# Stage two in nine chunks of 512 tokens, and seven own buffers for the last layer's values

## The chip, the cores and the metric

The kernel runs on one NeuronCore of one Trainium2 chip. The metric is the device time of one execution, in microseconds (us). Five engines matter: TensorE (PE; its weight loads are listed apart as PEld), VectorE (DVE), ScalarE (ACT), GpSimd (POOL) and SyncE (SP), which here issues most of the DMA transfers in the order of its queue.

## What is computed

Linear attention with random features over 8 batches, 8 heads and 576 tokens of 64 numbers, and a gated layer on its output, 4608 tokens of 512 numbers:

```python
def phi(x):                                   # x of q or k, scaled by D**-0.25
    h = np.einsum('bhsd,md->bhsm', x, omega) - np.sum(x * x, axis=-1, keepdims=True) / 2.0
    return np.exp(h - np.max(h, axis=-1, keepdims=True)) / np.sqrt(m)
kv  = np.einsum('bhsm,bhsd->bhmd', k_p, v);  z = np.sum(k_p, axis=2)
num = np.einsum('bhsm,bhmd->bhsd', q_p, kv)
den = np.einsum('bhsm,bhm->bhs', q_p, z)[..., None] + 1e-06
x   = (num / den).transpose(0, 2, 1, 3).reshape(4608, 512)
out = (1 / (1 + np.exp(-(x @ w_gate))) * (x @ w_val)) @ w_out   # 512 -> 1536 -> 512
```

## The kernel before

Every product of the gated layer is made of three matmuls: each operand is split into a rounded high part and the rest (a low part), and high x high, high x low and low x high are added up in PSUM. The high part is a copy by ScalarE, the low part a subtraction by VectorE or GpSimd.

Stage one holds the attention and, interleaved with it by a planner, the first 4 of the 12 column tiles of the gated layer (line 531), in chunks of 512 tokens, the first of them in two of 256. There the weights `wh`, `wl` are the stationary operand and the tokens `xe` the moving one. Results go to DRAM as `ye`, the attention's output as `xT`.

Stage two (`second_pass`, line 689) does the other 8 column tiles, in 4 pairs, by a seven-product scheme for 2 x 2 blocks (Strassen-Winograd). It runs over `NCW` = 6 chunks of `NW` = 768 tokens, in two halves of `W` = 384. For each pair there are two groups (`kind` 0 the gate, 1 the value), so n = 0 to 7 in a chunk. A group (`gated`, line 615) is seven products of six matmuls at line 631, stationary `units` (weights, `u`), moving `x` (token sums, `xl`), 128 x W each, in three of the eight PSUM banks. PE's order is 1, 6, 5 of a group, then 4, 3 of the group before (`held`), then 2, 7 of the group. Between the products stand their sums out of PSUM: line 645 copies the first result to `p1`, line 613 adds on VectorE (`u2` after product 6, `u3` and one more after product 7, one each after 4 and 3), lines 639 and 654 are the sigmoids, line 652 the one multiplication on VectorE, which comes once per pair. Products 2, 7, 4 and 3 write again into banks from which a sum has to be read first. After a pair's second group GpSimd makes seven operations (line 680) for the seven operands of the last layer, and two DMAs (line 687, `put`) store them to `yl`, issued by SP in the next pair's second group.

The next chunk's seven operands are made during a chunk by `operands` (line 582): four loads into `xr` when n = 1 is done, and then sums (line 591), high parts (line 577) and low parts (line 580) at places written out as (chunk, n, slot); most of them come at n = 7 and at n = 0 of the chunk itself. There are eight buffers for them (`buffer`, line 432): seven in the pool `late`, one in the pool `tail`. In the last chunk the units of the last layer are loaded as the units of stage two come free (line 442, one per group from n = 1 to n = 6), and `first_values` puts the loading and splitting of the first token group's values there.

The last layer (`last`, line 777) goes over 18 token groups of 2 x 128 tokens. For each of six pairs j it takes raw values of 128 x 896 (`gated_values`: for j below 2 three loads from `ye`, line 734, and four sums, line 741; otherwise one load from `yl`, line 736), splits them (`parts_of`, lines 749 and 751) into `yh` and `yl`, which lie `APART` floats into two of the same eight buffers, and runs 21 matmuls at line 800, stationary `yh`/`yl`, moving `u`, 128 x 256. So a group has 126. Raw values sit in buffers of the tags `xr` and `ya`, two of each, shared with stage two; of the first group's six, the last four are in a buffer of the tag `u`. The first matmuls of group 0 run ahead of products 4 and 3 of stage two's last group. At the end of each token group line 816 copies a result and line 613's sums give the output.

`BELOW`, `APART` and the tiles that nothing uses move tiles in memory by so many floats.

Of the kernel before, what the change touches and what calls it, by code (L numbers as in the profile page):

```python
# [9 lines left out]
F32 = mybir.dt.float32  # L10
# [10 lines left out]
P = 128  # L21
# [14 lines left out]
NC = 512  # L36
Q = NC // 2
NCH = B * S // NC
W = 3 * P
NW = 2 * W  # L40
NCW = B * S // NW
SUB = W // P
NJ = DF // P
NPAIR = NJ // 2
# [7 lines left out]
BANKS, PAIRS = 4, 2  # L52
XK = 6
XL, XE = 7, 1
UL, UE = 5, 3


BELOW, APART = 80, 80

FILL = 1e6  # L60

# [25 lines left out]
N_OPS = 7  # L87
# [142 lines left out]
def attn_glu_kernel(ctx: ExitStack, tc, qT, kT, qn, kn, va, om, ident, w, out):  # L230
# [30 lines left out]
    def any_bank(name):  # L261

        n_banks[0] += 1
        return bank(n_banks[0] % 8, name)
# [5 lines left out]
    def pin(ins):  # L270
        return tc.keep_in_program_order(ins) if pinned else ins
# [39 lines left out]
    def after(event, t):  # L311
        while event.left:
            yield event
        return max(t, event.time)
# [4 lines left out]
    def dve(n):  # L319
        return (n + 65) / 0.96  # L320
# [10 lines left out]
    def dma(t, kb, n=1):  # L331

        turns.free["SP"] = t + n * ISSUE
        moved[0] = max(moved[0], t + n * ISSUE + LANDS) + kb * 3.2
        return moved[0]
# [94 lines left out]
    turn_of = [0]  # L430

    def buffer(name):
        at, n = (late, XL) if turn_of[0] % (XL + XE) < XL else (tail, XE)
        turn_of[0] += 1
        return at.tile([P, 2, 2, W], F32R, tag="x", bufs=n, name=name)

    def unit(pool, n):
# [144 lines left out]
    def operands(c, x):  # L582

        xr = [tail.tile([P, 2, NW], F32, tag="xr", bufs=2, name=f"xr{c}_{i}") for i in range(2)]
        for k in range(KC):
            pin(nc.sync.dma_start(out=xr[k // 2][:, k % 2], in_=xT[k, :, c * NW : (c + 1) * NW]))
        (a11, a21), (a12, a22) = ((r[:, :, :W], r[:, :, W:]) for r in xr)
        s = late.tile([P, 2, W], F32, tag="s", bufs=1, name=f"s{c}")

# [25 lines left out]
    def gated(c, x, pair, kind, g, ya, yb):  # L615
# [3 lines left out]
        wh, wl = units[2 * (pair - EP) + kind]  # L619
        b0, b1, b2 = (any_bank(f"gw{i}_{id_}")[:, :W] for i in range(3))  # L620
        v0, v1, v2 = (b.rearrange("p (s t) -> p s t", s=SUB) for b in (b0, b1, b2))
# [101 lines left out]
        assert not plan  # L723
        return held

    def gated_values(g, j, raw=None):

        if raw is None:
            raw = tail.tile([P, 8, P], F32, tag=("xr", "ya")[j % 2], bufs=2, name=f"yr{g}_{j}")
        t = g // SUB * NW + g % SUB * P  # L730
        if j < EP:
            one, two, both = ye[j, :, 1, t + W : t + W + P], ye[j, :, 0, t + W : t + W + P], ye[j, :, :, t : t + P]
            for to, x in ((raw[:, :2], both), (raw[:, 2], one), (raw[:, 7], two)):
                pin(nc.sync.dma_start(out=to, in_=x))
        else:
            pin(nc.sync.dma_start(out=raw[:, :N_OPS], in_=yl[j - EP, :, g]))
        return raw

    def sums(raw, pin=lambda x: x):
        for o, a, b, op in ((4, 7, 2, ALU.add), (3, 4, 0, ALU.subtract), (5, 0, 7, ALU.subtract), (6, 1, 3, ALU.subtract)):  # L740
            pin(nc.vector.tensor_tensor(out=raw[:, o], in0=raw[:, a], in1=raw[:, b], op=op))  # L741

    def parts_of(g, j, raw, pin=lambda x: x):
        yh, yl_ = (
            buffer(f"{t}{g}_{j}").rearrange("p a b t -> p (a b t)")[:, APART : APART + N_OPS * P].rearrange("p (o t) -> p o t", t=P)
            for t in ("yh", "yl")
        )
        x = raw[:, :N_OPS]
        pin(nc.scalar.activation(out=yh, in_=x, func=AF.Copy))  # L749
        engine = nc.gpsimd if j == NPAIR - 1 and g else nc.vector  # L750
        pin(engine.tensor_tensor(out=yl_, in0=x, in1=yh.bitcast(F32), op=ALU.subtract))  # L751
        return yh, yl_

    first, ahead = {}, []

    def first_values():

        raws = [gated_values(0, j, tail.tile([P, 8, P], F32, tag="xr", bufs=2, name=f"yr0_{j}")) for j in range(2)]

        def parts(j):  # L760
            first[j] = parts_of(0, j, raws[j], pin)

        def others():
            both = tail.tile([P, NPAIR - 2, N_OPS, P], F32, tag="u", bufs=UE, name="yr0_2")
            raws.extend(gated_values(0, j, both[:, j - 2]) for j in range(2, NPAIR))
            first["raws"] = raws

        c = NCW - 1
        return {
            (c, 2, 2): [lambda: sums(raws[0], pin)],  # L770
            (c, 3, 2): [lambda: sums(raws[1], pin)],
            (c, 7, 0): [lambda: parts(0)],
            (c, 7, 1): [others],
            (c, 7, 2): [lambda: parts(1)],
        }

# [350 lines left out]
    late = tail = None  # L1127
    stores = []
    with tc.tile_pool(name="early", bufs=1) as early, tc.tile_pool(name="keep", bufs=1) as keep:
        with tc.manual_schedule():  # L1130
            with (
                tc.tile_pool(name="a", bufs=1, side="right") as a_pool,
                tc.tile_pool(name="two_banks", bufs=1, space=bass.MemoryType.PSUM) as two_banks,
            ):
                pool = a_pool
                for key, rank in sorted(order.items(), key=lambda x: x[1]):
                    n, *a = key
                    if n[0] == "n":
                        u, b = a
                        sqs[n[1], u, b] = pool.tile([P, MID + 1, H, 3], F32, tag="sq", bufs=4 * U, name=f"sq{n[1]}{u}_{b}")  # L1140
                        if (u, b) in OWN:
                            continue
                        turns.start(norms(pool, n[1], *a, {"k": kn, "q": qn}[n[1]]), rank)
                    else:
                        turns.start({"k": keys, "q": queries}[n](pool, *a), rank)
                for j in range(NE):
                    turns.start(first_weights(j), FIRST_RANKS[j])
                for n in range(N_LATE):
                    turns.start(late_weights(n), LATE_RANKS[n])
                turns.start(chunk_loads(), -1)  # L1150
                turns.start(products(), 2 * FILL)
                turns.run(lambda: not attended[0] and not unstored[0])
            late = ctx.enter_context(tc.tile_pool(name="late", bufs=1, side="right"))
            other_banks = ctx.enter_context(
                tc.tile_pool(name="other_banks", bufs=1, space=bass.MemoryType.PSUM)
            )
            for n in range(UL):
                turns.start(early_unit(n), 3 * FILL)
            result = {}

            def first_operands():
                x = {}
                for n in (0, 4, 3, 1, 5, 2, 6):
                    b = buffer(f"xl0_{n}")
                    x[n] = b[:, 0], b[:, 1]
                result["x"] = x
                a = {n: x[n][1].bitcast(F32) for n in x}
                t = yield from after(x_ready[-2][-1], 0)
                t = yield "SP", t, None, None
                for n, k, o in ((0, 0, 0), (5, 0, W), (2, 2, W), (1, 2, 0)):  # L1170
                    for i in range(2):
                        nc.sync.dma_start(out=a[n][:, i], in_=xT[k + i, :, o : o + W])
                t = dma(t, 1536, 8)
                s = late.tile([P, 2, W], F32, tag="s", bufs=1, name="s0")
                for n, p, q, op in (
                    (3, a[5], a[2], ALU.add), (4, s, a[0], ALU.subtract), (6, a[1], s, ALU.subtract),
                    (5, a[0], a[5], ALU.subtract), (0, None, None, None), (1, None, None, None), (2, None, None, None),
                ):
                    y = a[n] if op is None else s
                    if op is not None:  # L1180
                        t = yield "DVE", t, None, "S"
                        nc.vector.tensor_tensor(out=s, in0=p, in1=q, op=op)
                        t = use("DVE", t, dve(2 * W), LAG, "S")
                    t = yield "ACT", t, None, None
                    nc.scalar.activation(out=x[n][0], in_=y, func=AF.Copy)
                    t = use("ACT", t, act(2 * W), LAG)
                    t = yield "DVE", t, None, "S"
                    nc.vector.tensor_tensor(out=x[n][1], in0=y, in1=x[n][0].bitcast(F32), op=ALU.subtract)
                    t = use("DVE", t, dve(2 * W), LAG, "S")

            turns.start(first_operands(), 0.0)
            turns.run(lambda: not turns.live)
    tail = ctx.enter_context(tc.tile_pool(name="tail", bufs=1))
# [75 lines left out]
```

## Time and profile before

| what | value |
|---|---|
| median of 3 runs | 1090.72 us |
| the runs | 1074.8, 1090.72, 1091.19 us |
| profiled execution, its own time | 1090.43 us |
| its span | 1088.7 us |
| mean granted clock of TensorE | 0.988 |

The span goes from the first to the last instruction of the profiled execution. The page gives each engine's busy time, its share of the span and its number of instructions; the costliest groups (line, engine, operation, result<-operands, shape, count, busy time, mean of one in ns, idle time before and who ended it); the chain of work that ended last; and DMA issues. Other views answer for one stretch of time (busy time of each engine, granted clock, share of the DMA engines, GB/s), for one engine's instructions in order of time (start, duration, line, operation), and for waits. A matmul's duration covers its way through the array, so that durations of neighbours overlap.

### The profile page before, as it was taken

Reading aid. Unit: us, or ns where it says so; the run is one execution under the profiler, and the core shown is the slowest. Engines: PE = TensorE matmul, PEld = TensorE weight load, DVE = VectorE, ACT = ScalarE, POOL = GpSimd, SP = SyncE. Lnnn points to the kernel's source line nnn. Section 1 sums busy time; section 2 is a strip of 40 time slices with the busy share of each in tenths; the row PEclk is TensorE's granted clock in tenths of the full one; section 3 lists DMA queues with packets and bytes.
Section 4 is the critical chain, followed back from the end, with each engine's and each line's share of the span. In section 5 each row is a group of like instructions: output and inputs, shape, how many; then the busy total and the mean of one; then the engine's idle time right before and its main releaser. Section 6 shows DMA issues by size and latency. Waiting matters only on the chain.

```text
span 1088.7 us, 26466 instructions
## 1 busy us (share of the span) xinstructions
PE 1057.5 (97%) x10556; PEld 983.2 (90%) x10556; DVE 772.8 (71%) x1482; ACT 490.9 (45%) x1026; POOL 406.6 (37%) x326
## 2 busy tenths in 40 slices
PE   6789999999999999999999999999999899999998
PEld 5678888878878878899999999999999899999998
DVE  3989998998888856457647575747657767666664
ACT  6677756866555445343323232323233444443442
POOL 0341532342343422126756576766543111111111
PEclk9889999999999999999999999999999999999999
DMA  7588979998768648152324234142896666666663
GB/s 281 181 269 272 322 251 345 322 332 281 264 208 297 215 161 314 49 220 89 123 103 159 103 111 151 65 168 81 323 384 203 195 196 202 192 196 193 195 197 104
DMA packets 121323, 226.32 MB, mean 208 GB/s; under 512 B 10992, under 2 KB 59888, under 8 KB 118128
## 3 DMA queue, kind: packets, MB, share of 16 engines
q1 hardware_dynamic: 115872, 215.39, 58.5%
q10 hardware_dynamic: 5328, 9.24, 2.3%
q8 instruction: 83, 1.36, 0.5%
q14 instruction: 40, 0.33, 0.1%
HBM read 144.90 MB, written 79.69 MB: 206 GB/s over the span
## 4 chain that ended last, share of the span: by engine, by line
PE 88%; DVE 5%; issue 2%; DMA 2%; ACT 1%; POOL 1%; SPq 0%; DVEq 0%; POOLq 0%; ACTq 0%
PE gw L631 32%; PE po L800 23%; PE gv L531 15%; PE pkv L1004 4%; PE ppq L922 3%; PE ppk L922 3%; PE pnq L1069 3%; PE ptq L1052 3%; PE pxq L1094 1%; ACT kpk L980 1%; POOL xe L507 1%; DVE hq L1034 1%; DVE xq L1086 1%; DVE sqq L929 0%; DMA yr<-yl 0%
## 5 line engine op out<-in xcount | busy, mean ns | idle before, releaser
L631 PE MATMUL gw<-xl,u 128*128 128x384 f32 x2016 | 350.4, 334 | 0.0
L631 PEld LDWEIGHTS gw<-xl,u 128*128 128x128 f32 x2016 | 349.2, 188 | 0.9 <-issue 0.9
L800 PE MATMUL po<-u,yh 128*128 128x256 f32 x1512 | 268.4, 282 | 0.0
L800 PEld LDWEIGHTS po<-u,yh 128*128 128x128 f32 x1512 | 232.1, 189 | 0.0
L800 PE MATMUL po<-u,yl 128*128 128x256 f32 x756 | 213.4, 282 | 3.1 <-DVE yl L751 3.1
L531 PE MATMUL gv<-xe,wh 128*128 128x512 f32 (+1 forms) x640 | 191.2, 378 | 1.0 <-POOL xe L507 1.0
L749 ACT ACTIVATE yh<-yr 128x896 fp32r<-128x896 f32 x108 | 102.4, 953 | 160.2 <-PE po L800 108.4
L800 PEld LDWEIGHTS po<-u,yl 128*128 128x128 f32 x756 | 145.5, 192 | 3.7 <-DVE yl L751 3.7
L531 PEld LDWEIGHTS gv<-xe,wh 128*128 128x128 f32 x640 | 114.4, 189 | 21.4 <-POOL xe L507 1.9
L751 DVE TENSOR_TENSOR yl<-yr,yh 128x896 fp32r<-128x896 f32 x91 | 101.5, 1121 | 41.4 <-ACT yh L749 41.3
L531 PE MATMUL gv<-xe,wl 128*128 128x512 f32 (+1 forms) x320 | 120.9, 378 | 0.3 <-DVE xq L1086 0.3
L751 POOL TENSOR_TENSOR yl<-yr,yh 128x896 fp32r<-128x896 f32 x17 | 36.1, 2124 | 217.6 <-ACT yh L749 204.9
L613 DVE TENSOR_TENSOR u<-gw,p 128x384 f32<-128x384 f32 x96 | 53.3, 555 | 67.0 <-PE gw L631 45.8
L680 POOL TENSOR_TENSOR ya<-ya,g 128x384 f32<-128x384 f32 x48 | 60.0, 1251 | 96.2 <-issue 43.2
L639 ACT ACTIVATE g<-g 128x384 f32<-128x384 f32 x72 | 37.8, 526 | 109.9 <-DVE g L613 109.9
L507 POOL TENSOR_TENSOR xe<-xr,xe 128x512 fp32r<-128x512 f32 (+1 forms) x40 | 51.5, 1310 | 91.9 <-ACT xe L498 91.8
L980 ACT ACTIVATE kpk<-ppk,nbk 128x128 f32<-128x128 f32 x256 | 71.9, 393 | 11.9 <-DVE nbk L938 11.6
L741 DVE TENSOR_TENSOR yr<-yr 128x128 f32<-128x128 f32 x144 | 47.3, 369 | 36.5 <-DMA yr<-ye 35.3
L531 PEld LDWEIGHTS gv<-xe,wl 128*128 128x128 f32 x320 | 60.3, 188 | 10.3 <-issue 0.5
L929 DVE TENSOR_REDUCE sqk<-ppk 128x8 f32<-128x1024 f32 (+1 forms) x48 | 45.2, 954 | 20.3 <-PE ppk L922 20.3
L929 DVE TENSOR_REDUCE sqq<-ppq 128x8 f32<-128x1024 f32 (+1 forms) x48 | 45.5, 956 | 17.7 <-PE ppq L922 17.6
L1057 ACT ACTIVATE qpq<-ptq 128x512 f32<-128x512 f32 (+1 forms) x80 | 41.5, 559 | 35.9 <-PE ptq L1052 35.7
(227 smaller groups left out, 1563.5 us busy)
## 6 DMA issues: line engine op xcount, KB each, us to landing
yr<-yl SPq DMA_DIRECT2D x72, 448.0 KB, 3.9
yl<-ya SPq DMA_DIRECT2D x24, 768.0 KB, 3.5
yl<-yb SPq DMA_DIRECT2D x24, 576.0 KB, 4.4
u<-w_parts SPq DMA_DIRECT2D x6, 1792.0 KB, 9.5
v<-va SPq DMA_DIRECT2D x32, 330.0 KB, 5.1
out<-o ACTq DMA_DIRECT2D x34, 256.0 KB, 2.4
natq<-qn SPq DMA_DIRECT2D x32, 256.0 KB, 5.1
xT<-xsq SPq DMA_DIRECT2D x64, 128.0 KB, 3.0
```

The lines of the kernel that those rows point to most:

```text
L507: nc.gpsimd.tensor_tensor(out=x[:, 1], in0=raw[:, k], in1=x[:, 0].bitcast(F32), op=ALU.subtract)
L531: nc.tensor.matmul(gv, lhsT=u[:, s], rhs=v, start=(m == 0), stop=(m == 3 * KC - 1))
L613: return nc.vector.tensor_tensor(out=o, in0=a, in1=b, op=ALU.add)
L631: nc.tensor.matmul(o, lhsT=u[:, k, s], rhs=v[:, kc, :], start=(first and m == 0), stop=(m == 5), skip_group_check=not first,)
L680: pin(nc.gpsimd.tensor_tensor(out=o, in0=a, in1=b, op=op))
L741: pin(nc.vector.tensor_tensor(out=raw[:, o], in0=raw[:, a], in1=raw[:, b], op=op))
L749: pin(nc.scalar.activation(out=yh, in_=x, func=AF.Copy))
L751: pin(engine.tensor_tensor(out=yl_, in0=x, in1=yh.bitcast(F32), op=ALU.subtract))
L800: nc.tensor.matmul(o, lhsT=u[:, i, :], rhs=v[:, k, :], start=(j + m == 0 and n in (1, 6, 5, 3)), stop=(j == NPAIR - 1 and m == 2), skip_gr ...
L922: nc.tensor.matmul(pp[r, h, k, :], lhsT=raw[HALVES[h], o + r.start : o + r.stop], rhs=om_sb[HALVES[h], :], start=True, stop=True,)
L929: nc.vector.tensor_reduce(out=z[:, :, :, 0], in_=pp, axis=AX.X, op=ALU.max)
L980: nc.scalar.activation(out=kp[t][:, h, :], in_=pp[:, h, i, :], func=AF.Exp, bias=nb[:, h, i : i + 1],)
```

## The change

Stage two takes nine chunks of 512 tokens in halves of 256, so `SUB` is 2 and there are still 18 token groups. The last layer's raw values get a tag of their own, `yr`, with seven buffers; all six of the first group are loaded where `first_values` is called, when n = 1 of the last chunk is done. Two unused tiles, `above_x` (16 floats) after the x tiles of the pool `late` and `below_x` (112 floats) ahead of the one in `tail`, are added, and `APART` goes from 80 to 32 floats.

```diff
-W = 3 * P
+W = 2 * P
...
+YS = 7
...
-BELOW, APART = 80, 80
+BELOW, ABOVE_X, BELOW_X, APART = 80, 16, 112, 32
...
     def buffer(name):
         at, n = (late, XL) if turn_of[0] % (XL + XE) < XL else (tail, XE)
         turn_of[0] += 1
+        if turn_of[0] == XL + 1:
+            tail.tile([P, BELOW_X], F32, name="below_x")
         return at.tile([P, 2, 2, W], F32R, tag="x", bufs=n, name=name)
...
-    def gated_values(g, j, raw=None):
-
-        if raw is None:
-            raw = tail.tile([P, 8, P], F32, tag=("xr", "ya")[j % 2], bufs=2, name=f"yr{g}_{j}")
+    def gated_values(g, j):
+
+        raw = tail.tile([P, 8, P], F32, tag="yr", bufs=YS, name=f"yr{g}_{j}")
...
-        raws = [gated_values(0, j, tail.tile([P, 8, P], F32, tag="xr", bufs=2, name=f"yr0_{j}")) for j in range(2)]
+        first["raws"] = raws = [gated_values(0, j) for j in range(NPAIR)]
...
-        def others():
-            both = tail.tile([P, NPAIR - 2, N_OPS, P], F32, tag="u", bufs=UE, name="yr0_2")
-            raws.extend(gated_values(0, j, both[:, j - 2]) for j in range(2, NPAIR))
-            first["raws"] = raws
...
-            (c, 7, 1): [others],
...
                     x[n] = b[:, 0], b[:, 1]
+                late.tile([P, ABOVE_X], F32, name="above_x")
                 result["x"] = x
```

## The prediction

> **What bounds the kernel now.** I read the totals first, then the costliest groups, the table by stretches, the chain, and last single rows.
>
> ```profile
> span 1088.7 us, 26466 instructions
> PE 1057.5 (97%) x10556; PEld 983.2 (90%) x10556; DVE 772.8 (71%) x1482; ACT 490.9 (45%) x1026; POOL 406.6 (37%) x326
> PE gw L631 32%; PE po L800 23%; PE gv L531 15%; PE pkv L1004 4%; PE ppq L922 3%; PE ppk L922 3%; PE pnq L1069 3%; PE ptq L1052 3%; PE pxq L1094 1%; ACT kpk L980 1%; POOL xe L507 1%; DVE hq L1034 1%; DVE xq L1086 1%; DVE sqq L929 0%; DMA yr<-yl 0%
> ...
> L631 PE MATMUL gw<-xl,u 128*128 128x384 f32 x2016 | 350.4, 334 | 0.0
> L800 PE MATMUL po<-u,yh 128*128 128x256 f32 x1512 | 268.4, 282 | 0.0
> ```
>
> The profiled execution took 1090.43 us, 1.7 more than its span, and 0.3 less than the median of 1090.72; the runs shown reach down to 1074.8, a gap I come back to. TensorE sets the end: lines 631 (stage two) and 800 (the last layer) hold 55% of the chain, and the change touches just these. By stretches (columns: length; busy time of PE, PEld, DVE, ACT, POOL; clock; DMA share; GB/s):
>
> ```profile
> 462.00:810.00 348.00, 348.00 (x2006) 347.13 (x2005) 215.21 (x322) 104.77 (x194) 211.49 (x176) 1.00 0.42 156
> 770.00:807.00 37.00, 37.00 (x215) 37.00 (x214) 20.46 (x36) 8.12 (x16) 20.08 (x20) 1.00 0.99 384
> 809.60:1083.00 273.40, 270.28 (x2273) 269.68 (x2272) 182.39 (x349) 105.79 (x125) 47.22 (x24) 0.99 0.64 193
> 855.00:860.00 5.00, 4.96 (x29) 0.66 0.80 276
> ```
>
> Stage two has no idle PE; VectorE and GpSimd are busy six tenths of it. Near its end the DMA engines are full (0.99). The last layer takes 273.4 us. So the price of one matmul from start to start decides, not the 334 or 282 ns of its duration, which overlap. I take that step from rows that recur:
>
> ```profile
> 706.93 0.56 DVE L652 TENSOR_TENSOR ya<-gw,g 128x384 f32<-128x384 f32 x1 [0.36 <-PE gw L631]
> 736.05 0.56 DVE L652 TENSOR_TENSOR ya<-gw,g 128x384 f32<-128x384 f32 x1 [0.41 <-PE gw L631]
> ...
> 904.74 0.37 ACT L816 ACTIVATE p1o<-po 128x256 f32<-128x256 f32 x1
> 1053.14 0.37 ACT L816 ACTIVATE p1o<-po 128x256 f32<-128x256 f32 x1
> ...
> 111.11 0.28 PE L531 MATMUL gv<-xe,wl 128*128 128x256 f32 x1
> 113.63 0.28 PE L531 MATMUL gv<-xe,wl 128*128 128x256 f32 x1
> ...
> 846.22 0.28 PE L800 MATMUL po<-u,yl 128*128 128x256 f32 x1
> 852.00 0.28 PE L800 MATMUL po<-u,yl 128*128 128x256 f32 x1
> ...
> 277.58 1.09 PE ptq L1052 x10
> ```
>
> Line 652 comes once per pair of column tiles: two pairs, 168 matmuls, 29.12 us, so **173.3 ns** for 384 columns. Line 816 comes once per token group of the last layer: ten groups of 126, 148.40 us, **117.8 ns** for 256 columns. Stage one's 256-wide matmuls: 21 in 2.52 us, **120.0**. And the same line 800 ran 51 in 5.78 us, **113.3**, in one stretch after a stop. The last row is ten transposes, each with its own 128x128 weight load: **109 ns**, about the pace of the loads. So the step of a 256-wide matmul isn't fixed by its shape.
>
> **What each part costs.** *Chunks of 512.* Stage two's 6 x 8 x 42 = 2016 matmuls become 9 x 8 x 42 = 3024 of 256 columns. Before: 2016 x 173.3 = 349.4 us. After: 329.6 at 109, 342.7 at 113.3, 356.2 at 117.8, 362.9 at 120.0. The trace has no 256-wide matmul of this line; these are the two sides, -19.8 and +13.5.
>
> *The pads.* In the compiled kernel all tiles around lie in multiples of 512 bytes, so stage two's weight columns (u) and moving columns (x) begin at the same place modulo 512 bytes, as in stage one; in the last layer weights (yh, yl) begin 320 bytes (APART = 80 floats) past the moving u. After: 16 floats above the x tiles push them down by 64 bytes, 112 floats below the single one in the other pool come to the same place (448 = 512 - 64), and yh, yl start at APART = 32 floats. Weights then stand 64 bytes past the moving operand in both stages. Distance 0 goes with 120.0; distance 320 with 117.8 and, for 51 steps, 113.3. 64 is unseen, in either stage: 109 to 120. These ends lie apart; their middle is 114.5, and the nearest row is 113.3. I take it for both: stage two 342.7 - 349.4 = **-6.7**, last layer 2268 x (113.3 - 117.8) = **-10.1**. One thing more speaks for it: 1090.7 - 1074.8 = 15.9 us, and a last layer wholly at 113.3 without its waits (4.2, below) would save 14.3. That the short run was this is a guess.
>
> The Trainium skill, "TensorE: Matmul & The Clock Gate", section "Back-to-back issue gap", gives a warm gap of N/2.4 + 2.5 ns, and its "Step-by-step" section says that loading the next weights takes no SBUF bandwidth from the running matmul. By that, an estimate, 256 columns cost 109.2 and 384 cost 162.5, and stage two would change by 3024 x 109.2 - 2016 x 162.5 = +2.6 us, with the pads inert. The trace disagrees on the step (120.0, 173.3); whether pads matter is the first rival.
>
> *Chunk boundaries*, 8 instead of 5, with less cover. VectorE just before and after a boundary (PE starts the chunk at about 693.1), and GpSimd beside it:
>
> ```profile
> 693.28 0.56 DVE L613 TENSOR_TENSOR u<-gw,p 128x384 f32<-128x384 f32 x1 [0.48 <-PE gw L631]
> ...
> 694.35 1.52 DVE L580 TENSOR_TENSOR xl<-xr,xl 128x768 fp32r<-128x768 f32 x1
> 695.90 2.48 DVE L591 TENSOR_TENSOR xr<-xr,xr 128x768 f32<-128x768 f32 x1
> 698.31 0.55 DVE L613 TENSOR_TENSOR u<-gw,p 128x384 f32<-128x384 f32 x1
> ...
> 699.70 3.21 DVE L580 TENSOR_TENSOR xl<-xr,xl 128x768 fp32r<-128x768 f32 x2
> 702.84 0.55 DVE L613 TENSOR_TENSOR u<-gw,p 128x384 f32<-128x384 f32 x1
> ...
> 695.01 2.56 POOL L580 TENSOR_TENSOR xl<-xr,xl 128x768 fp32r<-128x768 f32 x1
> 697.53 1.73 POOL L680 TENSOR_TENSOR ya<-ya,g 128x384 f32<-128x384 f32 x1
> ...
> PEld gw L631 <- issue: 0.9, 5, 0.2
> ...
> 708.56 2.48 SPq L586 DMA_DIRECT2D xr<-xT  x4
> L613 DVE TENSOR_TENSOR o<-po,u2o 128x256 f32<-128x256 f32 x18 | 7.5, 415 | 0.0
> ```
>
> Between the two u3 sums (693.28 and 702.84) VectorE queues six large operations that take turns with GpSimd's: the 2.48 is some 0.8 of work behind GpSimd's operation. The second u3 ends at 703.39; product 4, queued on PE to overwrite that bank, is due 10 products after the start, 693.1 + 10 x 1.04 = 703.5. It is hit already: 0.2 us of PEld at each of 5 boundaries. Scaled to 256 and 512 elements (0.56 to 0.42; 0.81 to 0.54; GpSimd's 0.9 and 1.7 to 0.63 and 1.17, by these rows' slopes), the second u3 ends 7.4 us after the start, and PE can go on at 7.55. Product 4 is due at 10 x 6 x 113.3 = 6.8. I take 0.7 per boundary (0.2 to 1.2): 8 x 0.7 - 0.65 = **+5.0** (+1 to +9).
>
> SP's queue stays in its order: the stores of line 687 wait for GpSimd's list, and the four loads of the next chunk (line 586) stand behind them, issued 15.5 us after the boundary. Scaled by three quarters, like GpSimd's list, that is 11; with 2.5 of issue and some 2.5 to land (two thirds of the bytes) they are there at about 16, when the first sum on them is due, at the end of the chunk's third group. If they are late, VectorE's queue stops, but PE asks for its next sum only some 3 us later. I cost it at nothing; without that cover, up to 1 us per chunk.
>
> *The last layer's own buffers.*
>
> ```profile
> 844.94 1.08 DVE yl L751
> ...
> 846.63 1.61 SPq L734
> ...
> 848.29 2.67 DMA yr<-ye
> ...
> 851.06 2.61 DVE yr L741 x3
> ...
> 855.03 7.07 PE po L800 x45
> ...
> 764.13 0.36 SPq L687 DMA_DIRECT2D yl<-ya  x1
> 765.70 4.69 SPq L734 DMA_DIRECT2D yr<-ye  x6
> 807.93 2.82 SPq L736 DMA_DIRECT2D yr<-yl  x4
> ...
> yl<-ya SPq DMA_DIRECT2D x24, 768.0 KB, 3.5
> yl<-yb SPq DMA_DIRECT2D x24, 576.0 KB, 4.4
> u<-w_parts SPq DMA_DIRECT2D x6, 1792.0 KB, 9.5
> ```
>
> Here a buffer comes free at 846, its loads land, three sums and a split follow, and PE has waited 2.5 us; then the clock stands at 0.66 for a while. All such loss: 273.4 - 2268 x 0.1178 - 12 x 0.1733 (stage two's last matmuls) = 4.2 us. Seven buffers take out this wait for a buffer. What is late next is the DMA: the last chunk moves six units of 1792 KB, now in 38 us, not 58, and these ran at 384 GB/s with the engines full. The stores ahead of them began 12.6 us after the boundary at 751.5 (764.13), so about 9.5 now; the first group's ten loads follow, 7 us of SP's issue by these rows so the units' data start at about 19. Units (11.0 MB) and the two pairs' stores between them (1.8 MB, two thirds of the KB shown) need 33 us: the last unit is there at about 52 and due at 51, and group one's first values queue behind it, with three sums, a copy and a split still to do. I estimate 3 us of waits (0 to 6): **-1.2** (-4 to +2).
>
> Sum: -6.7 - 10.1 + 5.0 - 1.2 = -13.0, so 1077.4 us.
>
> **Rivals.** *The pads do nothing or harm* (the slower side): stage two at stage one's 120.0, the last layer left at 117.8. +13.5, boundaries 8 x 0.3 - 0.65 = +1.8, -1.2: 1104.5. For it: the clean 120.0 with the same order of operands; 117.8 is what nearly all of line 800 shows. Against: the operands did show 113.3. It decides from a step of about 116 ns in both stages: 616.5 us for both before, less 3.8 of other costs, over 5292 matmuls. The page's rule has this sign, with a smaller loss. With 117.8 in both it gives +6.8 + 3.4 - 1.2: 1099.4.
> *No conflict at all*: 109 in both, -19.8 - 19.9; boundaries then cost more (due at 6.5, so 1.0 each, +7.4) and the full DMA adds some 3: 1061. For it: the transposes' pace; against: no 256-wide row has it.
> *The boundaries take it back*: 1.5 us each, if GpSimd gets one turn more before u3: 113.3 throughout, 1084.
> *The loads aren't early*: behind SP's stores and the units they are no earlier where it counts, 6 us of waits instead of 3: 1080.5. These last two lie inside the forecast's spread.
>
> **How the numbers follow.** Forecast with the two small rivals, 1069 to 1087: 0.42. Between, or 117.8 in both, 1087 to 1102: 0.27. 1102 and above: 0.11. Below 1069: 0.20. The range 1058 to 1103 leaves out about 0.07 below and 0.10 above; the likeliest case alone is 1069 to 1087. 2% of 1090.7 is 21.8, about what a measurement of this kernel tells from no change: faster (below 1068.9) 0.20, slower (above 1112.5) 0.05, same 0.75.
>
> **What would show it.** Line 652 recurs every 84 x 113.3 = 9.5 us within a chunk (9.9 or 10.1 in the rival); line 816 every 14.3 (14.84 unchanged if the pads are inert). A PE gap near product 4 after each of 8 boundaries, behind VectorE's u3. In the last layer no wait of SP for a buffer about 846; instead DMA full to the end of the units, and a short wait at group one. The prediction fails above all if the step isn't 113: each ns is 5.3 us.

## The result, and the profile after

The change makes the kernel slower: 1111.06 us (median of 4 runs, 1110.0 to 1115.0) against 1088.95 before (4 runs, 1074.8 to 1091.19), ratio 1.026 with a 95% interval of 1.021 to 1.031. (That ratio is not the quotient of these two medians, which is 1.020; beside the experiments below the kernel before took about 1082, and 1111.06 over that is 1.027.) The forecast was 1077.4; it missed by 34 us. The profiled execution took 1111.91 us, span 1110.1, so 21.4 more than the span before.

From the page after, the span and the rows that answer to those shown of before (busy time, mean ns | idle time before them and who ended it; for DMAs count, KB each, median time to landing):

```profile
span 1110.1 us, 29065 instructions
...
L635 PE MATMUL gw<-xl,u 128*128 128x256 f32 x3024 | 358.8, 281 | 12.8 <-DVE u L617 10.6
...
L797 PE MATMUL po<-u,yh 128*128 128x256 f32 x1512 | 268.6, 282 | 0.0
...
yl<-yb SPq DMA_DIRECT2D x36, 384.0 KB, 3.4
u<-w_parts SPq DMA_DIRECT2D x6, 1792.0 KB, 14.3
```

Stage two's matmuls now stand at line 635 and wait 12.8 us, where line 631 waited 0.0. The last layer (line 797) looks as it did. A unit takes 14.3 us to land, not 9.5. By stretches:

```profile
462.00:836.00 374.00, 361.18 (x3047) 356.80 (x3046) 240.94 (x482) 120.62 (x290) 231.20 (x270) 0.99 0.42 151
...
836.00:1105.00 269.00, 266.16 (x2247) 265.98 (x2247) 167.18 (x348) 102.56 (x122) 40.65 (x23) 0.99 0.63 190
```

From first to last start of its matmuls, without those of the other stage in between, stage two takes 371.3 us against 350.1 before, the last layer 271.5 against 272.2. So the loss lies in stage two: **+21.2 us**, in four parts. The first is the step. A window without a wait gives it as its length plus one matmul's duration (0.28), over the number of matmuls in it; columns as above, PE alone:

```profile
553.00:583.00 30.00, 30.00 (x257) 1.00 0.37 128
753.00:783.00 30.00, 30.00 (x267) 1.00 0.41 142
```

That is 117.8 ns in one stretch and 113.4 in another, same line, same operands, same clock. Over stage two 1429 of some 2950 steps without a stop are of the fast kind (under 115.5) and the mean is 115.7, so 3024 x 115.7 = 349.8: **+0.3** against before's 349.4, not -6.7. The other three are stops. TensorE's own rows (start, duration; in brackets the idle time and who ended it):

```profile
474.70 7.09 PE L635 MATMUL gw<-xl,u 128*128 128x256 f32 x60 [1.45 <-DVE u L617]
...
512.14 39.98 PE L635 MATMUL gw<-xl,u 128*128 128x256 f32 x336 [0.24 <-DVE u L617]
552.37 7.89 PE L635 MATMUL gw<-xl,u 128*128 128x256 f32 x65 [0.25 <-DVE u L617]
...
785.42 5.60 PE L635 MATMUL gw<-xl,u 128*128 128x256 f32 x47 [0.42 <-POOL xl L584]
791.28 24.06 PE L635 MATMUL gw<-xl,u 128*128 128x256 f32 x210 [0.27 <-DVE u L617]
821.77 10.40 PE L635 MATMUL gw<-xl,u 128*128 128x256 f32 x63 [6.43 <-DVE u L617]
```

A wait costs its idle time, 0.16 of lost overlap (281 - 118 ns) and a first step of 0.22, about 0.1 more than usual. *Opening*: 474.70 is the first of five waits in the first chunk, 3.05 us idle together, **+4.4**. *Boundaries*: two waits each, 0.65 to 1.2 us together, 7.4 for eight against 0.65 before: **+6.8**. The first, 785.42, is at the second matmul of product 5 of the chunk's first group, for a low part that GpSimd makes: 3.9 of the 7.4. The second, 791.28, is at product 4, behind `u3`: 3.6. *Last chunk*: one stop of 6.43 at 815, and then 63 matmuls in 10.40 us, 163 ns each: 26 of them ran at 213 ns, half clock, **+9.5**. The granted clock there (TensorE alone; length, busy, clock, DMA share, GB/s):

```profile
822.00:827.00 5.00, 5.00 (x24) 0.50 1.02 409
```

The chain of waits names the causes:

```profile
465.53 4.70 DMA u<-w
...
470.92 0.69 DVE u L455
...
788.62 2.18 DVE xl L584 x2
790.80 0.35 DVE u L617
...
802.25 16.12 DMA yl<-yb
...
819.19 0.72 POOL yb L684
```

In the opening VectorE's queue stands at the split (line 455) of units 5 to 7, whose weights land at 470. At a boundary two low parts stand ahead of `u3` in VectorE's queue. What product 5 waits for is GpSimd's low part of the sum `s`, here after the change and then before it:

```profile
784.06 1.30 POOL L584 TENSOR_TENSOR xl<-s,xl 128x512 fp32r<-128x512 f32 x1 [2.27 <-ACT xl L581]
```

```profile
693.20 1.86 POOL L580 TENSOR_TENSOR xl<-s,xl 128x768 fp32r<-128x768 f32 x1 [3.49 <-ACT xl L577]
```

Before, it ended at 695.06, and its matmul began at 695.34: 0.28 us to spare. After, it ends at 785.36, and PE stands until then. In the last chunk a 384 KB store takes 16.12 us to land. The queue of SP shows why, and GpSimd what it holds up:

```profile
794.03 3.87 SPq L737 DMA_DIRECT2D yr<-ye  x6
797.94 2.60 SPq L739 DMA_DIRECT2D yr<-yl  x4
800.64 0.85 SPq L446 DMA_DIRECT2D u<-w_parts  x2
...
802.25 0.48 SPq L691 DMA_DIRECT2D yl<-yb  x1
```

```profile
818.51 0.72 POOL L684 TENSOR_TENSOR yb<-g,ya 128x256 f32<-128x256 f32 x1 [10.66 <-DMA yl<-yb]
```

The store stands behind the early values and two units of 1792 KB; `yb` has one buffer, so GpSimd's next writing of it waits 10.66 us, VectorE waits for GpSimd, PE for VectorE. The Trainium skill says ("DMA: Bandwidth & Descriptors", "Queues, rings and completion order") that each DMA engine consumes descriptors in ring order, though a later one may complete earlier; the 16.12 us behind the units fit that order. Last, group one of the last layer waits 3.1 us from start to start of PE's matmuls (848.42 to 851.54), as the prediction estimated.

### The profile page after: what moved, and what is told of

Same layout as the page of the kernel before. It is cut to its first block, busy times and chain, and to the rows that moved or that the text cites. A ratio compares the mean times of both kernels' runs of the same rounds, so it can differ in the third digit from the quotient of the medians.

```text
span 1110.1 us, 29065 instructions
## 1 busy us (share of the span) xinstructions
PE 1065.8 (96%) x11564; PEld 988.5 (89%) x11564; DVE 778.6 (70%) x1638; ACT 502.4 (45%) x1119; POOL 419.4 (38%) x419
## 4 chain that ended last, share of the span: by engine, by line
PE 80%; DVE 9%; issue 4%; DMA 3%; ACT 3%; POOL 1%; SPq 0%; DVEq 0%; POOLq 0%; ACTq 0%
PE gw L635 24%; PE po L797 24%; PE gv L535 15%; PE ppq L919 3%; PE pkv L1001 3%; PE ppk L919 3%; PE pnq L1066 3%; PE ptq L1049 3%; DVE xl L584 2%; DMA yl<-yb 1%; PE pxq L1091 1%; ACT kpk L977 1%; DVE u L617 1%; ACT xl L581 1%; DVE hq L1031 1%
## 5 line engine op out<-in xcount | busy, mean ns | idle before, releaser
L635 PE MATMUL gw<-xl,u 128*128 128x256 f32 x3024 | 358.8, 281 | 12.8 <-DVE u L617 10.6
L635 PEld LDWEIGHTS gw<-xl,u 128*128 128x128 f32 x3024 | 354.4, 190 | 17.2 <-DVE u L617 10.1
L797 PEld LDWEIGHTS po<-u,yl 128*128 128x128 f32 x756 | 142.8, 189 | 3.0 <-issue 3.0
L754 DVE TENSOR_TENSOR yl<-yr,yh 128x896 fp32r<-128x896 f32 x91 | 99.1, 1094 | 53.0 <-ACT yh L752 51.7
L535 PEld LDWEIGHTS gv<-xe,wh 128*128 128x128 f32 x640 | 114.5, 189 | 21.4 <-POOL xe L511 1.8
L617 DVE TENSOR_TENSOR u<-gw,p 128x256 f32<-128x256 f32 x144 | 60.7, 422 | 65.0 <-PE gw L635 40.0
L643 ACT ACTIVATE g<-g 128x256 f32<-128x256 f32 x108 | 43.7, 418 | 124.5 <-DVE g L617 124.5
L684 POOL TENSOR_TENSOR ya<-ya,g 128x256 f32<-128x256 f32 x72 | 62.6, 869 | 84.4 <-DMA xr<-xT 33.2
L535 PEld LDWEIGHTS gv<-xe,wl 128*128 128x128 f32 x320 | 60.3, 189 | 10.3 <-issue 0.5
L744 DVE TENSOR_TENSOR yr<-yr 128x128 f32<-128x128 f32 x144 | 37.7, 312 | 32.2 <-DMA yr<-ye 31.7
## 6 DMA issues: line engine op xcount, KB each, us to landing
u<-w_parts SPq DMA_DIRECT2D x6, 1792.0 KB, 14.3
```

The costliest lines, as they stand in the source:

```text
L535: nc.tensor.matmul(gv, lhsT=u[:, s], rhs=v, start=(m == 0), stop=(m == 3 * KC - 1))
L617: return nc.vector.tensor_tensor(out=o, in0=a, in1=b, op=ALU.add)
L635: nc.tensor.matmul(o, lhsT=u[:, k, s], rhs=v[:, kc, :], start=(first and m == 0), stop=(m == 5), skip_group_check=not first,)
L643: pin(nc.scalar.activation(out=g[i], in_=g[i], func=AF.Sigmoid))
L684: pin(nc.gpsimd.tensor_tensor(out=o, in0=a, in1=b, op=op))
L797: nc.tensor.matmul(o, lhsT=u[:, i, :], rhs=v[:, k, :], start=(j + m == 0 and n in (1, 6, 5, 3)), stop=(j == NPAIR - 1 and m == 2), skip_gr ...
```

## Experiments on the step

All ratios are to the kernel before, run on the same chip; there its medians were 1081.7 to 1083.4, its single runs 1075.2 to 1093.0. Neighbouring intervals overlap, and a profile shows one run: causes are read from traces. "Distance" is that between weights and moving columns modulo 512 bytes. Which of two steps a stretch of matmuls gets is called its draw below.

**Pads out of the changed kernel** (distance 0 in stage two):

```diff
-BELOW, ABOVE_X, BELOW_X, APART = 80, 16, 112, 32
+BELOW, APART = 80, 80
```

> The chunks and the seven buffers stay; the pads go, so stage two's weights and moving columns begin at the same place modulo 512 bytes (distance 0) and the last layer's 320 apart, as before the change. Theory one, the distance sets the step: stage two at stage one's 120.0 ns, 3024 x (120.0 - 115.7) = 13 us more, about 1124, and the last layer as it was. Theory two, the pads are inert: the same mixture of 113.4 and 117.8 ns, about 1111, within 2 us.

1117.65 us, ratio 1.031 (1.026 to 1.035). A window of stage two, PE alone:

```profile
594.00:626.00 32.00, 32.00 (x269) 1.00 0.38 134
```

32.28 / 269 = 120.0 ns, all through. So the pads are worth 4.3 ns a step against the changed kernel's profile, 13 us, and theory one holds for the step. Its time, about 1124, was too high: stage two rose by 5.0 only. The slower PE waits less at the boundaries (0.4 us each, not 0.9), 1 us less in the opening and 3 us less in the last chunk, so that much of the gain of a faster step is given back.

**Distance 64 in the last layer of the kernel before:**

```diff
-BELOW, APART = 80, 80
+BELOW, APART = 80, 16
```

> The kernel before with one number changed: yh and yl begin 64 bytes past the moving u instead of 320. Theory one, this distance is the good one and something else kept the last layer at 117.8 after the change: 2268 steps at 113.3, 10 us less, about 1079. Theory two, distance 64 is as 320: 117.8 throughout, about 1089, within 2 us.

1081.41, ratio 0.999 (0.996 to 1.003). The last layer, PE alone, first of the kernel before (320), then of this one:

```profile
860.00:1060.00 200.00, 200.00 (x1700) 1.00 0.66 196
```

```profile
860.00:1060.00 200.00, 200.00 (x1767) 1.00 0.68 206
```

117.8 ns against 113.3 in the profiles, 10 us over the layer, and yet equal times. Neither theory covers that; it fits that both kernels draw one of the two steps: this one's ten runs reach from 1076.6 to 1091.5, as before's. In this profile the layer ran at 117.8 until a stop of 2.5 us at 855, and then 1930 matmuls at 113.3; in the profile of before 1916 at 117.8 from 858. That would explain the spread of the kernel before, too, but none of its short runs was profiled.

**128 bytes in the last layer:** `APART = 32` in the kernel before.

> The kernel before with yh and yl 128 bytes past the moving u instead of 320. Theory one: two steps, 113.4 and 117.8, belong to every distance but 0, and which of them holds is drawn anew at each stop of PE: the time spreads as before's (1076 to 1091), ratio within 0.4% of 1. Theory two: some distances hold one step for good: 128 gives 113.4 or less throughout (1076 or less in every run) or 117.8 throughout (1088 or more in every run).

1090.13, ratio 1.004 (1.000 to 1.007), no run under 1085.6:

```profile
860.00:1060.00 200.00, 200.00 (x1688) 1.00 0.66 196
```

118.7 ns, a third value, which neither theory named. The runs are nearer theory two: none was short.

**The pads alone, and other distances, with 384 columns.** Four kernels: the kernel before with `ABOVE_X, BELOW_X, APART` of 16, 112, 96 (distance 64 in stage two, 320 in the last layer); 64, 64, 112 (256, 192); 32, 96, 96 (128, 256); 8, 120, 16 (32, 32).

> The kernel before, 384 columns and all buffers as they were, with the change's pads alone: stage two's weights 64 bytes past its moving columns, the last layer's 320 as before. Theory: a step is its columns (53.3 ns per 128) and a remainder of 13.3 ns at distance 0, and 6.7 or 11.1 ns at distance 64, whatever the width: 384 columns take 166.7 or 171.1 ns in place of 173.3, stage two 338 to 346 us in place of 350, the time 5 to 13 us less than before, ratio 0.988 to 0.996. Rival: the remainder is hidden under a longer matmul, or belongs to 256 columns alone: 173.3 stays, ratio 1.00 within 0.4%.

> As the run with the pads alone, at other distances: 256 bytes in stage two, 192 in the last layer. Theory: each distance has steps of its own; 0 has one (120.0 for 256 columns), 64 and 320 two (113.4, 117.8), 128 perhaps 118.7. If 256 acts as 0 and 192 as 64, stage two stays at 173.3 and the last layer draws 113.4 or 117.8: ratio 0.99 to 1.00. Rival: only whether the two begin together counts: 256 gives 166.7 or 171.1, ratio 0.988 to 0.996.

> The same with 128 bytes in stage two and 256 in the last layer. If 128 is a distance of its own with 118.7 for 256 columns, stage two takes 172.0 for 384, 3 us less than before; if the 118.7 was a draw like the others, 166.7 to 171.1. Last layer at 256: 120.0 if it acts as 0 (5 us more than its slow draw), 113.4 or 117.8 if it acts as 64.

> The same with 32 bytes in both stages. If the step depends on the distance in steps of 64, 32 acts as 0: 173.3 and 120.0, ratio about 1.005. If any distance but 0 will do, 166.7 to 171.1 in stage two and 113.4 or 117.8 in the last layer: ratio 0.988 to 0.996.

Ratios 1.001 (0.997 to 1.005), 1.006 (1.003 to 1.009), 1.011 (1.004 to 1.018), 1.005 (1.001 to 1.008). One run of the second took 2621 us, unexplained. Windows of PE alone, the last layer first and then stage two, of the four in this order:

```profile
865.00:1065.00 200.00, 200.00 (x1767) 1.00 0.68 206
500.00:700.00 200.00, 200.00 (x1134) 1.00 0.34 121
```

```profile
860.00:1060.00 200.00, 200.00 (x1701) 1.00 0.66 195
665.00:700.00 35.00, 35.00 (x204) 1.00 0.22 80
```

```profile
860.00:1060.00 200.00, 200.00 (x1669) 1.00 0.65 193
500.00:700.00 200.00, 200.00 (x1140) 1.00 0.33 117
```

```profile
860.00:1060.00 200.00, 200.00 (x1692) 1.00 0.66 197
665.00:700.00 35.00, 35.00 (x204) 1.00 0.28 100
```

| distance | 256 columns, ns | 384 columns, ns |
|---|---|---|
| 0 | 120.0 | 173.3 |
| 32 | 118.4 | 173.2 |
| 64 | 113.4 or 117.8 | 176.7 |
| 128 | 118.7 | 175.7 |
| 192 | 117.7 | |
| 256 | 120.0 | 173.2 |
| 320 | 113.3 or 117.8 | |

The theory that a remainder is saved whatever the width is wrong: at 64 bytes 384 columns get slower, 176.7. At 128 they get slower too, which neither value expected for that run allowed. 256 acted as 0 at both widths and 192 as the slow draw of 64, as that run's theory had it, though its ratio of at most 1.00 was too low; 32 acted as 0 at 384 columns but took 118.4 at 256. The pads help 256 columns only. Narrow halves cost 13 us (120.0 x 3024 against 173.3 x 2016) and the pads bring about that back. Most rows are one draw each; the first of these kernels is no slower than before though its profile has 6 us more in stage two, so its other runs may have drawn otherwise, there or in the last layer.

## Experiments on the last chunk

**A second yb:**

```diff
-                yb = tail.tile([P, SUB, 3, P], F32, tag="yb", bufs=1, ...)
+                yb = tail.tile([P, SUB, 3, P], F32, tag="yb", bufs=2, ...)
...
-        os = tail.tile([P, 2, 2, Q], F32, tag="yb", bufs=1, ...)
+        os = tail.tile([P, 2, 2, Q], F32, tag="ya", bufs=2, ...)
```

> Theory: the stop of 6.7 us in the last chunk and the 26 matmuls at half clock behind it come from one buffer: yb is single, its store is queued on SP behind the last chunk's loads and lands 16 us after its issue, and GpSimd's next writing of yb waits for it. With a second yb the stop and the slow matmuls go: 9.3 us less, about 1102, with GpSimd's longest wait for yl<-yb under 3 us; if the next store is as late, about 3 us of wait stay and the time is about 1105. Rival: PE stops there because the DMA engines are full and something else of the chunk (the loads of xr, the store of ya) is as late: the stop moves to another releaser and the time stays within 2 us of 1111.

1106.23, ratio 1.020 (1.015 to 1.026). PE's row after the stop, and the chain:

```profile
817.81 9.38 PE L635 MATMUL gw<-xl,u 128*128 128x256 f32 x66 [2.38 <-DVE u L617]
```

```profile
801.26 15.65 DMA yl<-ya
```

The stop falls from 6.43 to 2.38, but the store of `ya` is now the late one (15.65 us), half clock still follows, and the first groups of the last layer stop for 4.9 instead of 3.1 from start to start. So `yb` made the stop as long as it was, and the theory's second case holds, the next store being as late, with the 1105 that it gave; that another transfer steps in was the rival's point.

**Chunks and pads without the seven buffers** (`first_values` and `gated_values` as before the change):

> Chunks of 512 and the pads, without the seven buffers: the last layer's first values are loaded as before the change. Theory: stage two still loses its 12 us at the opening and the boundaries, but the values' ten loads no longer stand in SP's queue ahead of the units and of the yb store, so the stop of 6.7 us shrinks to about 5 (the yb store is late by the units alone), and the wait for a buffer at the last layer's first groups comes back (4.2 us in place of 3.1): about 1110. Rival, the early loads are what fills the queue: the stop goes altogether, 9 us less, about 1103. Second rival, the buffers bring the last layer more than its visible waits: over 1115.

1099.98, ratio 1.016 (1.009 to 1.024). Two rows of the chain:

```profile
797.63 11.65 DMA yl<-yb
...
824.40 8.87 DMA yr<-yl
```

The stop in the last chunk is 1.55 from start to start, but the last layer's first values land late and PE waits 7.8 there. So the rival was right on the stop, nearly, and the first theory on the wait that comes back, though it is twice the size. The time, near the rival's 1103, is in part luck: of the 14.7 us that this profile's span is shorter than the changed kernel's, 3.6 lie ahead of stage two, where nothing was changed, and 3.6 in the last layer, which drew 113.3 here.

**The seven buffers kept, four of the six loads where they were before the change; and the same with a second yb:**

```diff
-        first["raws"] = raws = [gated_values(0, j) for j in range(NPAIR)]
+        raws = [gated_values(0, j) for j in range(2)]
...
+        def others():
+            raws.extend(gated_values(0, j) for j in range(2, NPAIR))
+            first["raws"] = raws
...
             (c, 7, 0): [lambda: parts(0)],
+            (c, 7, 1): [others],
```

> The changed kernel with its seven buffers, but only the first two pairs' values loaded a chunk ahead; the other four are loaded where they were before the change. Theory one, the early loads lengthen the queue ahead of the yb store: the stop in the last chunk falls from 6.7 to about 1.5 us, as without the buffers, and the wait at the last layer's first groups grows from 3 to about 8. Theory two, the buffers alone reorder VectorE's queue in the last layer (eight sums of the next group ahead of the output's sums): where the last layer draws 113.4, PE still waits 0.3 to 1 us in most groups, and its 190 us from 890 to 1080 hold about 1600 matmuls, not 1679. Rival to two: it is the early loads that shift the order; with them late there is no wait in the later groups. Time: ratio about 1.02 either way.

> The run with the late loads, and a second yb. Theory: both causes of the last chunk's stop are gone, PE stops there for less than 1 us and no matmul runs at half clock in stage two, which then takes 361 to 363 us; what is left over the kernel before is the boundaries, the opening and the step. Ratio about 1.015. Rival: the units' loads alone (11 MB in 39 us) make the stores late, and a stop of 1.5 to 3 us stays with two buffers of yb as it did with the early loads.

1110.26, ratio 1.025 (1.019 to 1.032), and 1110.71, 1.025 (1.019 to 1.031). Stage two takes 364.1 and 363.9 us, 7 less than after the change, and from its boundary until the last layer begins the last chunk has no stop over 0.3 us; yet the times are the changed kernel's. The stop went, as the theories said, but at the last layer's first groups PE waits 8.2 and 10.0 us from start to start. So the first run's theory one holds on both waits, nearly, and the second's ratio of 1.015 does not come. The 62 us around the change of stage (length, PE busy, clock, DMA share, GB/s), of the changed kernel, of the one with a second `yb` alone, of the one without the buffers, and of these two; then 80 us of the kernel before:

```profile
793.00:855.00 62.00, 52.73 (x419) 0.89 0.90 337
```

```profile
793.00:855.00 62.00, 55.00 (x438) 0.92 0.93 344
```

```profile
789.00:851.00 62.00, 52.21 (x423) 0.94 0.91 333
```

```profile
795.00:857.00 62.00, 52.07 (x428) 0.94 0.94 347
```

```profile
795.00:857.00 62.00, 52.25 (x428) 0.92 0.95 350
```

```profile
775.00:855.00 80.00, 76.92 (x550) 1.00 0.82 296
```

PE lacks 9.3, 7.0, 9.8, 9.9 and 9.8 us, wherever the loads stand, and lacked 3.1 before the change. In the last kernel the wait sits in one place, a load of 15 us behind the units:

```profile
825.16 15.09 DMA yr<-yl
```

So `yb` and the early loads choose the place of the stop, but only the second `yb` alone made the sum of the waits smaller, by 2.3. Most likely they come from the transfers that must pass at this point; no run here made these fewer, so that is not shown. The DMA engines are full from about 800 to 835 in each; before the change they were full too (0.99 in the row 770 to 807 of the prediction), but beside a chunk of 58 us. Now the chunk is 39.

**What the seven buffers do later.** Rows of PE from 890 to 1080 of the last kernel, and of the one without the buffers; both drew 113.4:

```profile
890.00:1080.00 190.00, 186.96 (x1616) 1.00 0.65 191
```

```profile
890.00:1080.00 190.00, 190.00 (x1679) 1.00 0.68 202
```

With the buffers PE waits 0.2 to 1.0 us in nearly every group, 63 matmuls or 7 us less in this stretch; that holds for all five kernels with them that drew the fast step here, with early or late loads, and for the sum kernel below, whose values share three buffers of `ya`. 1616 is also what the changed kernel did there at 117.8 without a wait: with the seven buffers the fast step brings next to nothing. ScalarE shows how (with the buffers):

```profile
946.92 2.64 ACT L752 ACTIVATE yh<-yr 128x896 fp32r<-128x896 f32 x3 [5.83 <-DVE o L617]
```

It stands 5.83 us at its output DMA for VectorE's sums, which come after eight sums on the next group's values in VectorE's queue; three high parts follow in a row. At 117.8 the changed kernel's ScalarE waits 2.91 us at this place and PE not at all. That the order of the queue is the cause is read from the rows; it wasn't changed alone.

## Experiments on boundaries and opening

**The boundary's operations spread over more places:**

```diff
-            (c - 1, 7, 2): [parts(1, ...), parts(5, ...), combined(a12, a12, a11, ALU.subtract)],
-            (c, 0, 1): [parts(2, ...), parts(6, ...)],
+            (c - 1, 7, 2): [parts(1, ...), parts(5, ...)],
+            (c, 0, 0): [combined(a12, a12, a11, ALU.subtract)],
+            (c, 0, 1): [parts(2, ...)],
+            (c, 0, 2): [parts(6, ...)],
```

> The changed kernel with the boundary's six large operations spread over three places instead of two (the combined sum after the first product group of the chunk, parts 2 and 6 a place apart). Theory: the two waits per boundary (for u2 at product 7, for u3 at product 4, 0.4 to 0.7 us and 0.3 to 0.5 us each) are VectorE's queue of large operations ahead of its sums; with the operations further apart most of both goes: 4 to 6 us less than after the change, ratio to before about 1.021, and the rows of PE after a boundary show one wait under 0.3 us. Rival: the waits are GpSimd's turns on the shared work, which come wherever the operations stand: the waits move one product on and the time stays within 2 us.

1107.6, ratio 1.022 (1.018 to 1.027). The same two waits, though:

```profile
782.75 6.40 PE L635 MATMUL gw<-xl,u 128*128 128x256 f32 x54 [0.41 <-POOL xl L584]
789.48 2.78 PE L635 MATMUL gw<-xl,u 128*128 128x256 f32 x22 [0.33 <-DVE xl L584]
```

Both are now for the operands themselves: the first as before, at product 5 (the expectation has it at product 7 and for `u2`), the second for one of the two low parts that were moved. Where the changed kernel ran at 113.4 a boundary cost it 1.2 us, and it costs 1.3 here, so the theory falls and the rival is nearer. That the ratio is near the theory's 1.021 is luck: stage two's 3 us less come from the draw (mean step 114.0).

**Units 5 to 7 split a group later** (`2 + i // 3` for `1 + i // 3`):

> The changed kernel with the splits of the weight units 5 to 7 in stage two's first chunk one product group later. Theory: the five waits at 473 to 493 us (4.4 us) are VectorE held in these splits by weights that land only at 470; one group later the weights are there: 3 to 4 us less, ratio to before about 1.023. Rival: the splits themselves (not the wait for the weights) take VectorE's time, and the sums are as late one group on: the waits move by 5 us and the time stays.

1109.63, ratio 1.023 (1.018 to 1.028). The waits moved to 483 to 500 us:

```profile
483.74 3.01 PE L635 MATMUL gw<-xl,u 128*128 128x256 f32 x24 [0.30 <-DVE u L617]
...
498.69 11.50 PE L635 MATMUL gw<-xl,u 128*128 128x256 f32 x93 [0.53 <-DVE u L617]
```

Mostly the rival: the first wait of 1.45 went, but the splits themselves take VectorE's time, and 3.3 of the 4.4 us stay. The ratio is the theory's 1.023, but not by its way.

**All together, without the seven buffers** (both edits above, three buffers each of `ya` and `yb`):

> Chunks of 512 and the pads without the seven buffers (the run that came to a ratio of 1.016), with the boundary spread, the units' splits one group later, and three buffers each for ya and yb. Theory, the sum of the parts: 5 us for the boundaries, 3.5 for the opening, 2 to 3 for the stop in the last chunk: about 11 us less than that run, a ratio of about 1.006. What then keeps it from falling below the kernel before is the step: at 115.4 ns 256 columns cost what 384 cost at 173.3, and the boundaries bring nothing. Rival: a stop that goes lets the next one show (the late first values of the last layer, 7.8 us in that run, grow by what stage two gains): a ratio of 1.012 or more.

1107.9, ratio 1.023 (1.017 to 1.028): the rival. Stage two came to 360.8, its shortest, and the values of the last layer were late instead, behind

```profile
821.86 15.12 DMA yr<-yl
```

with a stop of 10.3 us from start to start. No version with nine chunks beats the kernel before.

## Why the prediction was wrong

- **The step is the term that failed first.** 113.3 was taken for both stages. Measured: a mean of 115.7 in stage two (+0.3, not -6.7) and 117.8 in the last layer (nothing, not -10.1). The row it rested on, 51 steps of line 800 at 113.3, was one of two values that the same instructions take, not the value of a distance; distance 64 has both, as 320 does. Even the fast value would not have brought the last layer's 10.1: three profiles with the seven buffers that drew it over most of that layer (pads out, spread operations, units later) are only 0.6 to 1.5 us shorter there. The rival of inert pads was wrong as well: without them stage two takes 120.0. Its 1104.5 came nearest, but by another way, +13.5 from the step.
- **The last layer's waits** were put at 3 us after the change, and group one's wait is 3.1. But the sum took the overflow of the last chunk only as late values. The same full DMA held back a 384 KB store, and so GpSimd, VectorE and PE, for 6.4 us in stage two, and half clock followed: +9.5, unpriced. "SP's queue stays in its order" was costed for the loads of `xr`, not for the stores behind the units. The working had it within reach: DMA full from 19 to 52 us after a boundary runs past a chunk of 39.
- **The opening** wasn't priced at all: +4.4. The splits of units 5 to 7 are in no row of the prediction.
- **Boundaries**: the wait at product 4, behind `u3`, was foreseen, and it costs 0.44 each instead of 0.7. The wait at product 5 for GpSimd's low part, 0.48 each, was not; there the kernel before had 0.28 us to spare. That the sum, +6.8, lies near +5.0 and within +1 to +9 is luck.
- **The buffers**: the last layer moved by 0.7 us, about the -1.2. That kernels with them lose some 7 us when the step is fast was not foreseen.
- **The guess on the short run** of 1074.8 is borne out in kind, not shown: with one distance changed the same layer drew the step 10 us lower at equal median times.

Measured sum: +0.3 + 4.4 + 6.8 + 9.5 in stage two (21.0 of 21.2), -0.7 in the last layer, +0.9 elsewhere.

## What to carry to other kernels

When a loop's chunks get shorter, set what must be transferred beside the last chunk against its new length: here TensorE stopped in every version, and more buffers mainly chose where. Price what stands once per run (openings, last chunks) and small stores behind large loads as carefully as the steady loop. Before a matmul's step is used in a sum, look in several stretches whether it has one value.

## What the runs showed of the hardware

The same matmuls ran at 113.4 or 117.8 ns at full granted clock. The switch came mostly at stops, in the changed kernel at one of 0.33 us from start to start (673 us), and in the kernel with the units later at a single step of 128 ns (989 us). Moving one operand in memory changes the step (table above, read as the distance of the two), at 64 and 128 bytes in opposite directions for 256 and 384 columns. What decides the draw stays open. After stops of 6.7 and 3.1 us from start to start the clock was halved (0.50 in the row above) for 26 and 16 matmuls, about 213 ns each. The Trainium skill ("TensorE: Matmul & The Clock Gate", "Back-to-back issue gap") gives a gap of N/1.2 ns for the slow clock, by that 213 for 256 columns as an estimate, which agrees. For the full clock its N/2.4 + 2.5, which the page gives for a matmul on its own, makes 109.2, which no stretch of pairs of weight load and 256-wide matmul reached here.
